# Projecting k and v of the second batch with half of the heads in either column tile of TensorE

## The chip, the cores and the metric

One core of a Trainium2 chip runs the whole program. The metric is the time of one execution in microseconds of device time; medians of several executions are given. "Before" is the kernel as it was, "the changed kernel" the one with the change. One profiled execution of each kernel gives the trace; its span is 1.7 to 1.8 us shorter than the timed figure of the same execution, so spans are compared with spans and times with times.

## The reference

```python
# q, k, v: (8 batches, 8 heads, 1024, 64); E, F: (64, 1024); FFN 512 -> 1536 -> 512
k_proj = einsum('ks,bhsd->bhkd', E, k)            # 64 projected keys per head
v_proj = einsum('ks,bhsd->bhkd', F, v)
attn   = softmax(q @ k_proj^T / sqrt(64))
x      = (attn @ v_proj), heads side by side      # (8192, 512)
out    = (silu(x @ w_gate) * (x @ w_val)) @ w_out # (8192, 512), float32
```

The matrix work is nearly all in the last line. The change is in the first two, for one batch out of eight.

## The kernel before

TensorE's order is written by hand. The feed-forward steps of one half batch (`gps`: gate, `vps`: value, `yps`: output) run in numbered slots; the attention of the *next* batch is put into some slots between them. Batch 0 is done in the prologue, batches 2 to 7 project k and v together, k in the left half of the array's columns and v in the right half. Batch 1 is the exception: its v arrives from memory much later than its k, so each is projected alone.

```python
def u_KV(b, what="kv", hs=(0, H), at="a"):
    ...
    todo = [x for x in (("k", 0, ET, kb), ("v", 64, FT, vb)) if x[0] in what]
    for j in range(NJ):                                   # 8 pieces of the sequence
        for _, lo, w, src in todo:
            nc.tensor.matmul(
                out=t[lo : lo + 64, h0:h1].rearrange("p h d -> p (h d)"),
                lhsT=w[:, j, :],                          # 128 x 64: half of the columns
                rhs=src[b][:, h0:h1, j, :],               # 8 heads x 64 = 512 columns
                start=(j == 0), stop=(j == NJ - 1),
            )
    if "k" in what:
        nc.scalar.copy(out=ks[b % 2][0:64, h0:h1], in_=t[0:64, h0:h1])
    ...                                                   # v: two VectorE copies into BDV

def u_KT(b, at="a", prs=(0, NPAIR)):                      # k' turned: 4 products of 64 columns
    for pr in range(*prs):
        nc.tensor.matmul(out=t[:, pr, :],
            lhsT=ks[b % 2][:, 2 * pr : 2 * pr + 2, :].rearrange("p h d -> p (h d)"),
            rhs=ident_bf[:, 0:KP], start=True, stop=True)
    ...                                                   # copies into the block diagonal BD

def u_TD(b, ch):                                          # q transposed by a DMA
    nc.sync.dma_start_transpose(out=t[:], in_=qb[b, ch][:].rearrange("p h j d -> p (h j d)"))
...
    if b == 1:
        put(22, u_TD, 1, 0)
        put(29, u_KV, 1, "k")
        put(32, u_KT, 1)
        put(40, u_KV, 1, "v")
        sa = (35, 36, 37, 38, 41, 42, 43, 44)             # slots of the scores
```

The prologue's loads go through GpSimd's DMA queue in program order:

```python
    load_v(0, (0, 4, 6, 8))
    load_w_gv(0, 1)            # gate and value weights, first block of 128 columns
    ...
    load_w_gv(10, 12)
    load_q(1, 0)
    load_k(1)
    load_wo(0)
    load_wo(1)
```

The softmax here doesn't subtract the row's maximum and nothing guards it: scores larger than these inputs give would overflow.

Of the kernel before, what the change touches and what calls it, by code (L numbers as in the profile page):

```python
# [12 lines left out]
BF16 = mybir.dt.bfloat16  # L13
FP32 = mybir.dt.float32
# [4 lines left out]
D = 64  # L19
# [3 lines left out]
P = 128  # L23
NJ = S // P
NPAIR = H // 2
# [9 lines left out]
def kernel(  # L35
# [19 lines left out]
    nc = tc.nc  # L55
    scale = 1.0 / float(D) ** 0.5

    const = ctx.enter_context(tc.tile_pool(name="const", bufs=1))
# [13 lines left out]
    ident_bf = const.tile([P, P], BF16, name="ident_bf")  # L72
    ident_fp = const.tile([P, P], FP32, name="ident_fp")
    BD = [const.tile([P, H, P], BF16, name=f"BD{i}") for i in range(2)]
    BDV = [const.tile([P, NPAIR, P], BF16, name=f"BDV{i}") for i in range(2)]
    ks = [const.tile([P, H, D], BF16, name=f"ks{i}") for i in range(2)]
    ET = const.tile([P, NJ, KP], BF16, name="ET")
    FT = const.tile([P, NJ, KP], BF16, name="FT")

# [4 lines left out]
    kb, vb, qb, xT, hT = {}, {}, {}, {}, {}  # L84
# [45 lines left out]
    kvp = {}  # L130
    banks = {"a": (ps_a, "pa"), "g": (ps_g, "gps"), "v": (ps_v, "vps"), "y": (ps_y, "yps")}

    def bank(where, shape, dt, name):
        pool, tag = banks[where]
        return pool.tile(shape, dt, name=name, tag=tag)

    def copy(eng, out, in_):
        (nc.scalar.copy if eng is nc.scalar else eng.tensor_copy)(out=out, in_=in_)  # L138

    def u_KV(b, what="kv", hs=(0, H), at="a"):  # L140
# [5 lines left out]
        h0, h1 = hs  # L146
        todo = [x for x in (("k", 0, ET, kb), ("v", 64, FT, vb)) if x[0] in what]
        for j in range(NJ):
# [15 lines left out]
        if h1 == H:  # L164
            kvp.pop(key)

    def u_V0(p0, p1, at):

        t = bank(at, [P, p1 - p0, P], FP32, "kvp")
        nc.tensor.matmul(  # L170
            out=t[:].rearrange("p a d -> p (a d)"),
            lhsT=zeros[:, 0:P], rhs=zeros[:, 0 : (p1 - p0) * P],
            start=True, stop=False,
        )
        src = vb[0][:].rearrange("p (a c) j d -> p a c j d", c=2)
        for j in range(NJ):
            for c in range(2):
                nc.tensor.matmul(
                    out=t[64 * c : 64 * c + 64, :, 64 * c : 64 * c + 64],
                    lhsT=FT[:, j, :],  # L180
                    rhs=src[:, p0:p1, c, j, :],
                    start=False,
                    stop=(j == NJ - 1),
                )
        nc.scalar.copy(out=BDV[0][:, p0:p1, :], in_=t[:])

    def u_V0w(p0, p1, at):
# [10 lines left out]
        for c in range(2):  # L198
            rows = slice(64 * c, 64 * c + 64)
            nc.scalar.copy(out=BDV[0][rows, p0:p1, rows], in_=t[64:P, :, c, :])  # L200

    def u_KT(b, at="a", prs=(0, NPAIR)):




        t = bank(at, [P, NPAIR, KP], FP32, "kTp")
        for pr in range(*prs):
            nc.tensor.matmul(  # L209
                out=t[:, pr, :],  # L210
                lhsT=ks[b % 2][:, 2 * pr : 2 * pr + 2, :].rearrange("p h d -> p (h d)"),
                rhs=ident_bf[:, 0:KP],
                start=True,
                stop=True,
            )
        bd = BD[b % 2][:].rearrange("p (a c) k -> p a c k", c=2)
        for c in range(2):
            src = t[64 * c : 64 * c + 64, slice(*prs)]
            nc.vector.tensor_copy(out=bd[0:64, slice(*prs), c, 0:64], in_=src)
            nc.vector.tensor_copy(out=bd[64:128, slice(*prs), c, 64:128], in_=src)  # L220
# [239 lines left out]
    def put(s, fn, *a):  # L460
        slots[s].append((fn, a))

    def place(b):
        s0 = 48 * (b - 1)
        if b == 1:
            put(22, u_TD, 1, 0)
            put(29, u_KV, 1, "k")
            put(32, u_KT, 1)
            put(40, u_KV, 1, "v")
            sa = (35, 36, 37, 38, 41, 42, 43, 44)  # L470
            put(41, u_AD, 1, 0)
            put(30, u_TD, 1, 1)
            put(47, u_AD, 1, 1)
            sp = (44, 45, 46, 46, 66, 67, 68, 69)
        else:
            put(s0 + (8 if b == 2 else 0), u_KV, b)
            put(s0 + (11 if b == 2 else 3), u_KT, b)
            o = 14 if b == 2 else 6
            put(s0 + (9 if b == 2 else -6), u_TD, b, 0)
            put(s0 + (11 if b == 2 else -4), u_TD, b, 1)  # L480
            sa = [s0 + o + 3 * j for j in range(NJ)]
            put(sa[3] + 4, u_AD, b, 0)
            put(sa[7] + 4, u_AD, b, 1)
            sp = [s0 + i for i in (39, 41, 43, 45, 57, 59, 61, 63)]
        for j in range(NJ):
            put(sa[j], u_S, b, j)
            put(sa[j] + 1, u_R, b, j)
            put(sa[j] + 1, u_N, b, j)
        for i in range(8):
            put(sp[i], u_PV, b, i // 4, i % 4)  # L490
# [5 lines left out]
    with tc.manual_schedule():  # L496
# [3 lines left out]
        for i in range(2):  # L500
            nc.scalar.dma_start(
                out=kraw[i][:],
                in_=k[0, 2 * i : 2 * i + 2].rearrange("h (p j) d -> p h (j d)", j=NJ),
# [12 lines left out]
        def turn(which, at, halves=(0, 1), eng=nc.scalar):  # L516
            for half in halves:
# [7 lines left out]
                js = slice(4 * half, 4 * half + 4)  # L525
                copy(eng, (ET, FT)[which][:, js, :], ps[:])

# [52 lines left out]
        u_A(0, 0, act)  # L580
        u_V0w(0, 2, "y")
        u_V0(2, 3, "v")
        u_PV2(0, 0, 0, 0, act)
        u_A(0, 2, dve)
        u_N(0, 3, dve)
        u_V0(3, 4, "y")
        u_PV1(0, 0, 2, 0, act)
        u_PV1(0, 0, 3, 0, act)
# [35 lines left out]
        for b in range(1, B):  # L624
            place(b)
        for b in range(2, B):
            s0 = 48 * (b - 1) - (20 if b == 3 else 24)
            at = (43, 43, 44, 45) if b == 2 else (s0, s0 + 2, s0 + 4, s0 + 6)
# [10 lines left out]
        for c in range(B * CH - 1):  # L639
            for n in range(NFT):  # L640
                f = n if c else 4 + (2 * n + 1) // 3
                ypart[(c + 1) * NFT + f].append((c, n))

        for t in range(NIT):
            c, f = divmod(t, NFT)
            i = 1 if t < 2 else None
# [39 lines left out]
```

## Time and profile before

| | before |
|---|---|
| time, median of 3 runs | 567.86 us (567.65 to 568.19) |
| span of the profiled run | 565.8 us |
| TensorE busy | 98%, granted clock 1.00 |
| k of batch 1, start to next work | 1.84 us |
| v of batch 1, start to next work | 1.84 us |
| turning k' | 0.11 us |

In a timeline line the first number is the start in us from the span's beginning, the second the length, then engine, source line, operation, tiles written and read, weight block, moving block and count; in brackets is the idle time before it and what ended it. Matmul records overlap, so the cost of a piece of TensorE work is read as the distance from its start to the start of the next. The prediction below shows the lines.

### The profile page before, as it was taken

How to read it: one execution, taken by the hardware profiler on the slowest of the kernel's cores; microseconds unless marked ns; L12 is line 12 of the kernel's file. 1: busy time of each engine (PE TensorE's matmuls, PEld its weight loads, DVE VectorE, ACT ScalarE, POOL GpSimd, SP SyncE). 2: the span in 40 equal slices, each digit the busy share in tenths (PEclk: the TensorE clock that was granted, in tenths of full speed). 3: DMA queues.
4: the chain of work that ended last, by engine and by line, in shares of the span. 5: the costliest groups of instructions: out<-in, count | busy, mean ns of one | idle time of the engine just before them, and what ended most of it. 6: DMA issues, size and time to landing. Idle time of an engine off the chain costs nothing.

```text
span 565.8 us, 7865 instructions
## 1 busy us (share of the span) xinstructions
PE 556.9 (98%) x2904; PEld 266.0 (47%) x2958; DVE 339.6 (60%) x579; ACT 235.7 (42%) x417; POOL 111.9 (20%) x126
## 2 busy tenths in 40 slices
PE   8999999999999999999999999999999999999997
PEld 4654444444444444444444444444444444444444
DVE  3786665766476655765566655666547665545550
ACT  3574352453444433543435434354343542443222
POOL 6860250133012400133002230024100220000000
PEclk9999999999999999999999999999999999999999
DMA  9999989629903795029920399005990213010012
GB/s 206 188 199 188 182 139 204 120 57 199 203 25 75 120 204 105 38 57 172 191 67 37 77 188 201 38 20 112 193 180 19 61 35 74 37 38 33 24 39 93
DMA packets 112215, 62.78 MB, mean 111 GB/s; under 512 B 66352, under 2 KB 103472, under 8 KB 112176
## 3 DMA queue, kind: packets, MB, share of 16 engines
q0 software_dynamic: 43952, 29.49, 36.5%
q1 hardware_dynamic: 67392, 31.46, 25.3%
q10 hardware_dynamic: 832, 1.31, 0.7%
q8 instruction: 23, 0.38, 0.3%
q14 instruction: 16, 0.13, 0.1%
HBM read 60.29 MB, written 16.78 MB: 136 GB/s over the span
## 4 chain that ended last, share of the span: by engine, by line
PE 95%; DMA 3%; issue 1%; ACT 0%; POOL 0%; POOLq 0%
PE vps L395 29%; PE yps L433 29%; PE gps L395 29%; PE kvp L150 3%; PE sc L286 2%; PE pv L343 2%; DMA wg<-in_moe_w_gate_dram 2%; DMA kb<-in_k_dram 2%; PE qTp L252 0%; PE kTp L209 0%; PE yps L395 0%; PE aTp L332 0%; ACT th L407 0%; ACT AT L138 0%; POOL qb L108 0%
## 5 line engine op out<-in xcount | busy, mean ns | idle before, releaser
L414 DVE SCALAR_TENSOR_TENSOR s<-th,gps 128x512 f32<-128x512 f32 x191 | 129.7, 679 | 134.0 <-ACT th L407 133.6
L395 PE MATMUL vps<-xT,wv 128*128 128x512 bf16 (+1 forms) x762 | 196.1, 377 | 0.9
L395 PE MATMUL gps<-xT,wg 128*128 128x512 bf16 (+1 forms) x750 | 193.9, 377 | 1.0
L433 PE MATMUL yps<-wo,hT 128*128 128x512 bf16 (+2 forms) x763 | 191.8, 376 | 0.7
L407 ACT ACTIVATE th<-gps 128x512 f32<-128x512 f32 x191 | 114.0, 597 | 159.9 <-PE gps L395 145.4
L419 DVE TENSOR_TENSOR hT<-s,vps 128x512 bf16<-128x512 f32 x192 | 131.9, 687 | 20.8 <-DVE s L414 0.5
L316 POOL TENSOR_TENSOR AAd<-ee,rr 128x512 bf16<-128x512 f32 x56 | 58.2, 1041 | 342.5 <-issue 221.7
L433 PEld LDWEIGHTS <-hT 128*128 128x128 bf16 x780 | 76.2, 98 | 89.9
L395 PEld LDWEIGHTS <-wv 128*128 128x128 bf16 x776 | 73.8, 98 | 83.6 <-issue 3.2
L395 PEld LDWEIGHTS <-wg 128*128 128x128 bf16 x776 | 74.0, 98 | 81.4 <-issue 0.8
L443 ACT ACTIVATE ysb<-yps 128x512 f32<-128x512 f32 (+1 forms) x65 | 38.4, 590 | 77.7 <-PE yps L433 75.5
L138 ACT CAST xT<-pv 128x512 bf16<-128x512 f32 (+1 forms) x63 | 36.2, 578 | 51.3 <-PE pv L343 50.3
L301 DVE TENSOR_REDUCE zz<-ee 128x8 f32<-128x512 f32 x64 | 43.5, 679 | 22.0 <-ACT ee L290 21.9
L290 ACT ACTIVATE ee<-sc 128x512 f32<-128x512 f32 x64 | 37.9, 596 | 19.1 <-PE sc L286 17.9
L286 PEld LDWEIGHTS <-qTd 128*128 128x128 bf16 x224 | 17.2, 98 | 13.2
L343 PE MATMUL pv<-AT,BDV 128*128 128x512 bf16 x60 | 22.4, 379 | 0.2
L286 PE MATMUL sc<-BD,qTd 128*128 128x128 bf16 x224 | 21.6, 219 | 0.1
L303 DVE RECIPROCAL rr<-zz 128x8 f32<-128x8 f32 x64 | 13.0, 203 | 6.3
L108 POOL DMA_DIRECT2D qb<-in_q_dram x18 | 16.3, 910 | 0.8 <-POOLq L670 0.8
L150 PE MATMUL kvp<-kb,ET 128*64 128x512 bf16 (+1 forms) x72 | 15.5, 358 | 0.0
L162 DVE CAST BDV<-kvp 64x256 bf16<-64x256 f32 x7 | 3.0, 426 | 20.0 <-ACT ks L158 17.8
L150 PE MATMUL kvp<-vb,FT 128*64 128x512 bf16 x56 | 13.4, 382 | 0.0
(74 smaller groups left out, 139.1 us busy)
## 6 DMA issues: line engine op xcount, KB each, us to landing
out_dram<-ysb SPq DMA_DIRECT2D x63, 256.0 KB, 2.3
qb<-in_q_dram POOLq DMA_DIRECT2D x14, 512.0 KB, 17.9
kb<-in_k_dram POOLq DMA_DIRECT2D x7, 1024.0 KB, 11.1
vb<-in_v_dram POOLq DMA_DIRECT2D x7, 1024.0 KB, 14.1
wo<-in_moe_w_out_dram POOLq DMA_DIRECT2D x2, 768.0 KB, 21.5
kraw<-in_k_dram ACTq DMA_DIRECT2D x2, 512.0 KB, 4.8
qb<-in_q_dram POOLq DMA_DIRECT2D x4, 256.0 KB, 7.8
wg<-in_moe_w_gate_dram POOLq DMA_DIRECT2D x4, 256.0 KB, 7.5
```

What stands on the lines that cost most here:

```text
L138: (nc.scalar.copy if eng is nc.scalar else eng.tensor_copy)(out=out, in_=in_)
L150: nc.tensor.matmul(out=t[lo : lo + 64, h0:h1].rearrange("p h d -> p (h d)"), lhsT=w[:, j, :], rhs=src[b][:, h0:h1, j, :], start=(j == 0), ...
L286: nc.tensor.matmul(out=ps[:, n, :], lhsT=t[:, n, :], rhs=BD[b % 2][:, 4 * g + n, :], start=True, stop=True)
L290: nc.scalar.activation(out=e[:].rearrange("p h j k -> p (h j k)"), in_=ps[:].rearrange("p a k -> p (a k)"), func=AF.Exp, scale=scale,)
L301: nc.vector.reduce_sum(out=z[:], in_=e[:], axis=AX.X)
L316: eng.tensor_tensor(out=a.rearrange("p j h k -> p h j k"), in0=ee.pop((b, u))[:], in1=rr.pop((b, u))[:].unsqueeze(3).to_broadcast([P, 4, 2 ...
L395: nc.tensor.matmul(out=ps[:, ts], lhsT=(wg, wv)[w][:, kt, f * P : (f + 1) * P], rhs=x[:, kt, ts], start=(kt == 0), stop=(kt == NKT - 1),)
L407: nc.scalar.activation(out=th[:], in_=ps[:], func=AF.Tanh, scale=0.5)
L414: nc.vector.scalar_tensor_tensor(out=s1[:], in0=th[:], scalar=1.0, in1=g[:], op0=ALU.add, op1=ALU.mult)
L419: nc.vector.tensor_tensor(out=hT[c][:, f, :], in0=s1[:], in1=ps[:], op=ALU.mult)
L433: nc.tensor.matmul(out=yy[c][:, cs], lhsT=hT[c][:, f, i * P : (i + 1) * P], rhs=wo[:, f, cs], start=(f == 0), stop=(f == NFT - 1),)
L443: nc.scalar.activation(out=ysb[:, cs], in_=yy[c][:, cs], func=AF.Copy, scale=0.5)
```

## The change

The eight heads are split into two sets of four. For each piece of the sequence, two matmuls of 256 columns follow each other, one for either set, with the same weights in the left and in the right half of the columns. If the halves run at the same time, a projection takes half as long. The heads of k' then lie on both row halves of a new tile `ksp`, so two products with the full identity turn it.

```diff
--- before.py
+++ after.py
@@ -74,6 +74,7 @@
     BD = [const.tile([P, H, P], BF16, name=f"BD{i}") for i in range(2)]
     BDV = [const.tile([P, NPAIR, P], BF16, name=f"BDV{i}") for i in range(2)]
     ks = [const.tile([P, H, D], BF16, name=f"ks{i}") for i in range(2)]
+    ksp = [const.tile([P, NPAIR, D], BF16, name=f"ksp{i}") for i in range(2)]
     ET = const.tile([P, NJ, KP], BF16, name="ET")
     FT = const.tile([P, NJ, KP], BF16, name="FT")
 
@@ -164,6 +165,39 @@
         if h1 == H:
             kvp.pop(key)
 
+    def u_K1(b, gs=(0, 2), at="a"):
+
+        g0, g1 = gs
+        t = bank(at, [P, 2 * (g1 - g0), D], FP32, "kvp")
+        src = kb[b][:].rearrange("p (g c e) j d -> p g c e j d", c=2, e=2)
+        for j in range(NJ):
+            for c in range(2):
+                nc.tensor.matmul(
+                    out=t[64 * c : 64 * c + 64].rearrange("p (g e) d -> p g e d", e=2),
+                    lhsT=ET[:, j, :],
+                    rhs=src[:, g0:g1, c, :, j, :],
+                    start=(j == 0),
+                    stop=(j == NJ - 1),
+                )
+        nc.scalar.copy(out=ksp[b][:, 2 * g0 : 2 * g1], in_=t[:])
+
+    def u_V1(b, at="a"):
+
+        t = bank(at, [P, NPAIR, D], FP32, "kvp")
+        src = vb[b][:].rearrange("p (a c) j d -> p a c j d", c=2)
+        for j in range(NJ):
+            for c in range(2):
+                nc.tensor.matmul(
+                    out=t[64 * c : 64 * c + 64],
+                    lhsT=FT[:, j, :],
+                    rhs=src[:, :, c, j, :],
+                    start=(j == 0),
+                    stop=(j == NJ - 1),
+                )
+        for c in range(2):
+            rows = slice(64 * c, 64 * c + 64)
+            nc.vector.tensor_copy(out=BDV[b % 2][rows, :, rows], in_=t[rows])
+
     def u_V0(p0, p1, at):
 
         t = bank(at, [P, p1 - p0, P], FP32, "kvp")
@@ -199,13 +233,22 @@
             rows = slice(64 * c, 64 * c + 64)
             nc.scalar.copy(out=BDV[0][rows, p0:p1, rows], in_=t[64:P, :, c, :])
 
+    def turn_ksp(t, b, g):
+        nc.tensor.matmul(
+            out=t[:, 2 * g : 2 * g + 2, :].rearrange("p a k -> p (a k)"),
+            lhsT=ksp[b][:, 2 * g : 2 * g + 2, :].rearrange("p h d -> p (h d)"),
+            rhs=ident_bf[:],
+            start=True,
+            stop=True,
+        )
+
     def u_KT(b, at="a", prs=(0, NPAIR)):
 
 
 
 
         t = bank(at, [P, NPAIR, KP], FP32, "kTp")
-        for pr in range(*prs):
+        for pr in range(*prs) if b > 1 else ():
             nc.tensor.matmul(
                 out=t[:, pr, :],
                 lhsT=ks[b % 2][:, 2 * pr : 2 * pr + 2, :].rearrange("p h d -> p (h d)"),
@@ -213,6 +256,8 @@
                 start=True,
                 stop=True,
             )
+        for g in range(2) if b < 2 else ():
+            turn_ksp(t, b, g)
         bd = BD[b % 2][:].rearrange("p (a c) k -> p a c k", c=2)
         for c in range(2):
             src = t[64 * c : 64 * c + 64, slice(*prs)]
@@ -464,9 +509,9 @@
         s0 = 48 * (b - 1)
         if b == 1:
             put(22, u_TD, 1, 0)
-            put(29, u_KV, 1, "k")
+            put(29, u_K1, 1)
             put(32, u_KT, 1)
-            put(40, u_KV, 1, "v")
+            put(40, u_V1, 1)
             sa = (35, 36, 37, 38, 41, 42, 43, 44)
             put(41, u_AD, 1, 0)
             put(30, u_TD, 1, 1)
```

## The prediction

> **What bounds the kernel now.** I read the page first: the busy shares, then the slices, then the chain that ended last.
>
> ```profile
> span 565.8 us, 7865 instructions
> ...
> PE 556.9 (98%) x2904; PEld 266.0 (47%) x2958; DVE 339.6 (60%) x579; ACT 235.7 (42%) x417; POOL 111.9 (20%) x126
> ...
> PEclk9999999999999999999999999999999999999999
> DMA  9999989629903795029920399005990213010012
> ...
> PE 95%; DMA 3%; issue 1%; ACT 0%; POOL 0%; POOLq 0%
> ```
>
> The reader is to see a core whose TensorE is occupied nearly all the time, at full clock, and whose end is set by TensorE for 95% of the chain; the 3% of DMA lies in the first 21 us (the long pieces of the chain in order of time: k until 10.8 us, a gate weight until 21 us). A busy TensorE is not by itself proof, as its records overlap, so I asked who made it wait. The view of waits, kept to TensorE, names five waits, all before 18 us, 2.6 us together; kept to the time after 52 us it is empty. So a microsecond of TensorE time removed after 52 us is a microsecond off the span, unless some other thing turns out to arrive too late for the earlier TensorE. The 40-slice row of the DMA shows where that could be: the transfer engines are full until some 64 us, just where the change works.
>
> Next the stretch that the change touches: the timeline of TensorE.
>
> ```profile
> 50.29 1.91 PE L150 MATMUL kvp<-kb,ET 128*64 128x512 bf16 x8
> 52.13 1.04 PE L395 MATMUL gps<-xT,wg 128*128 128x512 bf16 x3
> ...
> 54.74 0.28 PE L209 MATMUL kTp<-ident_bf,ks 128*128 128x64 bf16 x4
> 54.85 1.03 PE L395 MATMUL vps<-xT,wv 128*128 128x512 bf16 x4
> ...
> 67.93 1.91 PE L150 MATMUL kvp<-vb,FT 128*64 128x512 bf16 x8
> 69.77 1.04 PE L395 MATMUL vps<-xT,wv 128*128 128x512 bf16 x4
> ```
>
> Columns: start, length of the merged piece (to the end of its last matmul, so pieces overlap), engine, line, operands, weight block, moving block, count. The difference of two starts is what a piece costs: 52.13 - 50.29 = 1.84 us for k of batch 1, 69.77 - 67.93 = 1.84 us for v, 0.11 us for turning k'. Each projection is 8 matmuls of 512 columns whose weight block has only 64 columns: half of the array does nothing.
>
> **What the Trainium skill says.** (1) "TensorE: Matmul & The Clock Gate", Part 3, The mechanism: matmuls with tile positions in different column groups run at the same time, starting a few ns apart. The trace agrees. Batch 2 projects k and v together, one in either half of the columns:
>
> ```profile
> 94.08 0.40 PE L150 MATMUL kvp<-kb,ET 128*64 128x512 bf16 x1
> 94.08 0.40 PE L150 MATMUL kvp<-vb,FT 128*64 128x512 bf16 x1
> 94.32 0.38 PE L150 MATMUL kvp<-kb,ET 128*64 128x512 bf16 x1
> 94.32 0.38 PE L150 MATMUL kvp<-vb,FT 128*64 128x512 bf16 x1
> ```
>
> Pairs start within 0.01 us, and the sixteen last from 94.08 to 95.93, 1.85 us: no longer than the eight of batch 1. (2) The same page, Back-to-back issue gap: 262 cycles for 256 columns and 518 for 512, 109 and 216 ns at 2.4 GHz. The trace agrees at 512 (216 ns between starts above). At 256 the k of batch 0, whose heads come in halves, has it:
>
> ```profile
> 8.10 1.06 PE L150 MATMUL kvp<-kb,ET 128*64 128x256 bf16 x8
> 9.09 0.40 PE L252 MATMUL qTp<-ident_bf,qb 128*128 128x128 bf16 x4
> ```
>
> 9.09 - 8.10 = 0.99 us for eight; with one of them 0.27 us long, the other seven steps take (1.06 - 0.27)/7 = 0.11 us each. (3) "TensorEngine Tiling (Array Packing)", Overview, Key Properties: a change of tiling mode drains the engine. The four matmuls before k start at 49.33 and should give way at 49.33 + 4 x 0.216 = 50.19; k starts at 50.29. So about 0.1 us is lost on entry, in each of the two projections, before and after the change alike. (4) Its Restrictions: column tiling switches off the fast weight load. The trace agrees in the durations: a weight load of 64 columns takes 106 to 110 ns in these groups, one of 128 columns 98 ns. I return to it as a rival.
>
> **The change part by part.** k of batch 1: 8 matmuls of 512 columns go, 16 of 256 come, two by two in the two column tiles. Eight steps of 216 ns become eight steps of 111 ns (the batch 0 row): 8 x 0.105 = 0.84 us saved, 1.84 to about 1.00 us, all on the path. v of batch 1: the same, 0.84 us. Turning k': four matmuls of 64 columns, 0.11 us by the starts (54.85 - 54.74), become two of 128. A step of 128 columns is read from the scores: four cost 60.26 - 60.03 = 0.23 us, 56 ns each, so two are 0.11 us. Saved: 0.0; the new form is there because the heads now lie on both row halves. The sum on TensorE is 2 x 0.84 = 1.68 us.
>
> Beside the path: the ScalarE copy of k' goes from 64x512 (0.58 us at 52.24) to 128x256, which should be about 0.4 us by the 128x256 cast of batch 0 (409 ns). It has until 54.5 us before the turn needs it, so nothing is gained there. The two VectorE copies of v' keep their 64x256 form (0.43 us each); the two copies of the turned k' stay. No transfer, no buffer and no slot of the order changes; counting TensorE's instructions in the built kernels, 28 more (32 come with the projections, 4 go with the turn), with everything else in its order.
>
> **Where the saving meets something that does not move.** After k, TensorE comes 0.84 us earlier to the scores of batch 1, which need q transposed by a DMA.
>
> ```profile
> 40.69 7.11 SPq L264 DMA_TRANSPOSE qTd<-qb  x1
> ...
> 59.82 0.43 PEld L286 LDWEIGHTS <-qTd 128*128 128x128 bf16 x4
> 60.03 0.39 PE L286 MATMUL sc<-BD,qTd 128*128 128x128 bf16 x4
> ```
>
> That transposition was issued at 40.69 and landed 18.8 us later, in a time when the DMA engines are full: 59.5 us. Before the change that was 0.3 us ahead of the first weight load, so the trace shows no wait. After it the weight load would come at 59.82 - 0.84 = 58.98, while nothing in the change brings the transfer forward. I expect a new wait of about 59.5 - 59.0 = 0.5 us, less 0.1 for the weight load that otherwise runs ahead by 0.2 us and can be closer to its matmul: **0.4 us given back**. TensorE's order is fixed, so it is not made up elsewhere.
>
> The later meetings I worked out with a shift of 0.44 us before v and 1.28 us after it. Second q transposition: 65.18 + 4.3 = 69.5, needed at 71.51 - 1.28 = 70.2, enough. Transposition of the attention rows: issued at 69.26 after GpSimd's last product, landing 6.1 us later at 75.4; first needed at 76.72, which becomes 75.44. The issue comes 0.44 us earlier too, as it hangs on scores before v; but the DMA engines are full again from 67 to 73 us, so the landing may move less. Between 0 and 0.4 us; I take 0.05. The second half of the output weights lands at 33.39 + 23.5 = 56.9 and is used from 58.7, then 57.9: enough. v of batch 1 landed at 41.74 + 20.7 = 62.4, needed at 67.5 now: enough. From the loads of batch 2 on (issued from 74.73), issues follow TensorE's progress and everything is shifted alike.
>
> Sum: 567.86 - 1.68 + 0.40 + 0.05 = 566.6 us.
>
> **Rivals.** A: nothing arrives late, the whole 1.68 us is kept: 566.2. For it: the landing is one profiled execution's, and if it were 0.5 us earlier in the timed ones the wait is gone. Against: 0.3 us of room for 0.84 us of advance. B: the halves do not run two at a time, or the sixteen weight loads at about 110 ns bind: 16 x 0.11 = 1.76 us against 1.84, no gain, 567.8. For it: the slower weight load of column tiles. Against: batch 2 hides two per step, and v of batch 0 runs sixteen 64-column matmuls in alternating column tiles in 0.44 us, about 30 ns per pair, so weight loads of different tiles overlap at a far higher rate than is wanted here. C: the wait for q takes all of k's gain (landing half a microsecond later than recorded), or the attention rows take part of v's too: 567.0 to 567.3. D: VectorE or a PSUM buffer becomes the bound where TensorE runs ahead. Against: at both places VectorE stood idle for the projection (2.19 us before the copy of v'), and the copies it waits for now come earlier.
>
> **Range and chances.** Between A (566.2) and C (567.3) lies most of it; the three runs before span 0.54 us, so a median carries perhaps 0.25 us either way. Range 565.9 to 567.5. All of these are within 0.4% of the time before, and 2% would be 11 us: no path in the trace reaches it. Chances: faster by over 2% 0.003, within 2% 0.992, slower by over 2% 0.005.
>
> **What would show it right or wrong.** In the timeline: pairs of 128x256 matmuls starting within 0.01 us, 0.11 us apart, the next gate or value group 1.0 us after the first (B if 1.8). The turn: two matmuls of 128 columns in 0.11 us. In TensorE's waits after 52 us: one new line, scores waiting for the DMA of the transposed q, 0.2 to 0.6 us; if the list stays empty, A holds. Perhaps a second, PV waiting for the transposed attention rows. The sum is wrong if the landing of the first q transposition moves with TensorE, or if a later load loses its place among the transfers and is late for batch 2.

## The result, and the profile after

| | before | changed |
|---|---|---|
| time, median of 4 runs each, same rounds | 568.0 us (567.65 to 568.19) | 566.76 us (566.54 to 566.97) |
| span of the profiled run | 565.8 us | 564.7 us |
| k of batch 1 | 1.84 us | 1.00 us |
| v of batch 1 | 1.84 us | 0.99 us |
| turning k' | 0.11 us | 0.11 us |

The ratio is 0.9979 (95% interval 0.9962 to 0.9996). A ratio is the mean time of one kernel's fast runs over that of the other's in the same rounds, so it is not quite the ratio of the medians. The gain of about 1.2 us is smaller than the 1.68 us of TensorE time removed.

The timeline of TensorE in the changed kernel, at the places shown above for before:

```profile
50.88 1.06 PE L175 MATMUL kvp<-kb,ET 128*64 128x256 bf16 x16
51.88 1.04 PE L440 MATMUL gps<-xT,wg 128*128 128x512 bf16 x3
...
54.48 0.28 PE L237 MATMUL kTp<-ident_bf,ksp 128*128 128x128 bf16 x2
54.59 1.03 PE L440 MATMUL vps<-xT,wv 128*128 128x512 bf16 x4
...
67.67 1.06 PE L190 MATMUL kvp<-vb,FT 128*64 128x256 bf16 x16
68.66 1.04 PE L440 MATMUL vps<-xT,wv 128*128 128x512 bf16 x3
```

Sixteen matmuls take 51.88 - 50.88 = 1.00 us: by the single records the two of a pair start 0.003 us apart, a pair follows the one before after 0.106 us (the first after 0.13), and the gate matmul behind starts 0.205 us after the last pair, so some 0.1 us goes on leaving. The two products of the turn take 0.11 us as the four did. So the work itself shrank as worked out: 0.84 and 0.85 us.

But k starts at 50.88 us, where before it started at 50.29. TensorE lost 0.59 us before it reached the first changed instruction. From the start of k to the projections of batch 2 it is 42.09 us instead of 43.79, the full 1.70 us less; 1.70 - 0.59 is the 1.1 us between the two spans. So in this pair of traces all of the shortfall lies ahead of the change. The waits of TensorE in the changed kernel, longest first (engine, tile and line that waited, what it waited for, us in total, times, longest), show where:

```profile
PE warm L577 <- DVE zeros L555: 1.2, 1, 1.2
PE vps L440 <- DMA wv<-in_moe_w_val_dram: 0.8, 1, 0.8
PE sc L331 <- DVE BD L139: 0.7, 1, 0.7
```

The middle line is new: the first value matmuls waited 0.81 us for their weights, until 20.84 us. The timeline has them in before and then in the changed kernel:

```profile
19.91 0.60 PE L395 MATMUL vps<-xT,wv 128*128 128x256 bf16 x4
```

```profile
20.84 0.61 PE L440 MATMUL vps<-xT,wv 128*128 128x256 bf16 x4 [0.81 <-DMA wv<-in_moe_w_val_dram]
```

And the wait for q that the prediction expected is there, but only on the weight loads (the 0.31 us in the bracket below), where it costs nothing; kept to the time after 52 us, the list of TensorE's matmul waits is empty. The timelines of the weight loads and of TensorE's matmuls around the first scores:

```profile
59.75 0.23 PEld L331 LDWEIGHTS <-qTd 128*128 128x128 bf16 x4 [0.31 <-DMA qTd<-qb]
59.77 0.39 PE L331 MATMUL sc<-BD,qTd 128*128 128x128 bf16 x4
```

The scores would have started at 58.05 + 8 x 0.216 = 59.78 us behind the output products that began at 58.05; they started at 59.77. TensorE came late by itself, and so just in time for q, which was issued at 40.89 and took 18.8 us, landing at 59.7. Two candidates for the missing 0.4 to 0.5 us thus stood side by side: the landing of q (theory W), and the noise of the first 45 us, ahead of the change (theory N). Theory N was later split into P, the late start belongs to the program as built, and C, it is chance from run to run.

### The profile page after: what moved, and what is told of

It is laid out like the page before. It is cut to its first block, busy times and chain, and to the rows that moved or that the text cites. A ratio compares the mean times of both kernels' runs of the same rounds, so it can differ in the third digit from the quotient of the medians.

```text
span 564.7 us, 7892 instructions
## 1 busy us (share of the span) xinstructions
PE 555.2 (98%) x2917; PEld 266.0 (47%) x2972; DVE 339.5 (60%) x579; ACT 235.5 (42%) x417; POOL 111.9 (20%) x126
## 4 chain that ended last, share of the span: by engine, by line
PE 95%; DMA 2%; POOL 1%; issue 1%; ACT 0%; POOLq 0%
PE vps L440 29%; PE yps L478 29%; PE gps L440 29%; PE sc L331 2%; PE pv L388 2%; DMA wv<-in_moe_w_val_dram 2%; PE kvp L151 2%; POOL vb L100 0%; POOL qb L109 0%; PE kvp L175 0%; PE kvp L190 0%; PE qTp L297 0%; PE kTp L252 0%; PE yps L440 0%; POOL kb L90 0%
## 5 line engine op out<-in xcount | busy, mean ns | idle before, releaser
L139 ACT CAST xT<-pv 128x512 bf16<-128x512 f32 (+1 forms) x63 | 36.2, 578 | 52.3 <-PE pv L388 50.3
L151 PE MATMUL kvp<-kb,ET 128*64 128x512 bf16 (+1 forms) x64 | 13.6, 355 | 0.0
L151 PE MATMUL kvp<-vb,FT 128*64 128x512 bf16 x48 | 11.5, 382 | 0.0
```

The costliest lines, as they stand in the source:

```text
L139: (nc.scalar.copy if eng is nc.scalar else eng.tensor_copy)(out=out, in_=in_)
L151: nc.tensor.matmul(out=t[lo : lo + 64, h0:h1].rearrange("p h d -> p (h d)"), lhsT=w[:, j, :], rhs=src[b][:, h0:h1, j, :], start=(j == 0), ...
```

## The experiments

Twelve runs were made, of eleven new kernels and of the changed one again (e5). Each was profiled once and timed in five rounds (e11 has six times) beside before. Every one gave correct results. The 95% interval of a ratio of times is 0.7 us or more wide on either side, so a difference of 0.3 to 0.5 us between two kernels' times proves little by itself; such readings rest on the traces, one execution each. "Packed" means: in the new form.

**One table for all traces.** Three distances make the traces comparable. From the start of batch 2's projections to the end every trace has 471.70 to 471.77 us, so nothing after them matters. From the start of k of batch 1 to there, the kernels differ by what was edited and by waits. And the start of k itself differs. "Fetch" is explained below. PV is the product of the attention rows with v.

| kernel | k starts | k to batch 2 | waits before k, other than those of all traces | waits after k | fetch minus 1024th packet |
|---|---|---|---|---|---|
| before | 50.29 | 43.79 | none | none | +0.10 |
| changed | 50.88 | 42.09 | value weights 0.81 | none | -0.21 |
| e1, k only | 50.35 | 43.37 | none | q, 0.41 | -0.11 |
| e2, v only | 51.21 | 42.94 | value weights 0.85 | none | -0.16 |
| e3, changed, filled | 51.05 | 42.51 | value weights 0.73 | none | -0.22 |
| e4, before, filled | 50.46 | 44.22 | gate weights 0.23 | none | +0.16 |
| e5, changed again | 51.52 | 43.84 | E 1.1, half clock | q, 1.44; PV 0.3 | +0.59 |
| e6, before, padded | 50.66 | 43.78 | none over 0.3 | none | +0.18 |
| e7, k only, padded | 51.59 | 44.33 | E 1.1, half clock | q, 1.39 | +0.85 |
| e8, q early | 50.95 | 42.29 | value weights 0.66 | PV 0.2 | -0.28 |
| e9, changed, other v of batch 0 | 50.88 | 42.09 | value weights 0.93 | none | -0.13 |
| e10, v only, other v of batch 0 | 50.30 | 42.94 | gate weights 0.21 | none | -0.10 |
| e11, both edits | 52.35 | 43.09 | E 2.2, half clock | second q and PV, 1.0 | +0.95 |
| e12, before, finer warming | 51.07 | 43.79 | v of batch 0, 0.78 | none | -2.43 |

Waits after k are the distance to the same piece in a trace without a wait: from the start of k to the first scores it is 8.89 us with k packed, and from v to the first PV 7.94 us with v packed.

**e1 and e2: one half of the change each.** e1 puts v back, e2 puts k and its turn back.

```diff
# e1
-            put(40, u_V1, 1)
+            put(40, u_KV, 1, "v")
# e2
-            put(29, u_K1, 1)
+            put(29, u_KV, 1, "k")
-        for pr in range(*prs) if b > 1 else ():
+        for pr in range(*prs):
-        for g in range(2) if b < 2 else ():
+        for g in ():
```

> Only k of batch 1 (and its turn) packed. Theory W (the landing of the transposed q, near 59.5 to 59.8 us, takes part of k's gain): the trace shows k in 1.00 us instead of 1.84, a weight load of the scores waiting for the DMA of q, and the time falls by about 0.4 us against before. Rival N (the whole 1.68 us counts, and the missing 0.4 us is the noise of the first 45 us): it falls by 0.84 us.

> Only v of batch 1 packed, k and its turn as before. Theory W and rival N both say 0.84 us less than before, since nothing between v and the end is late; so v alone should be worth about twice k alone under W, and the same as k under N.

e1: 567.37 us (567.18 to 567.55) against 567.93 us of before (9 runs): 0.56 us less, ratio 0.9989 (0.9976 to 1.0001): the times alone can't tell 0.4 from 0.84. Its trace shows the wait that was predicted. The timeline of TensorE in e1:

```profile
57.52 1.89 PE L478 MATMUL yps<-wo,hT 128*128 128x512 bf16 x8
59.66 0.40 PE L331 MATMUL sc<-BD,qTd 128*128 128x128 bf16 x4 [0.26 <-DMA qTd<-qb]
59.90 1.03 PE L440 MATMUL gps<-xT,wg 128*128 128x512 bf16 x4
```

The scores could have started at 57.52 + 1.73 = 59.25 us and started at 59.66: 0.41 us lost of the 0.84 us that k gained. (The bracket says 0.26 because the modelled end of the last matmul before is later than the slot in which the next could have begun.) From k to batch 2 it is 43.37 us against 43.79: 0.42 us kept. Theory W is shown in this trace.

e2 was a miss under both theories: 567.63 us (567.35 to 567.69), only 0.30 us less by the medians where 0.84 was due; ratio 0.9993 (0.9980 to 1.0005). In its trace the work is right, 42.94 us from k to batch 2 against 43.79, 0.85 us less. But k starts at 51.21 us, 0.92 us later than in before, and the list of waits again has the first value weights, 0.85 us. So something ahead of every changed instruction differed, and in all five timed runs the gain was short.

**e3 and e4: filling the wait.** Two 512-column matmuls on a tile of zeros stand ahead of the first scores of batch 1, in the changed kernel and in before.

```diff
+        if (b, u) == (1, 0):
+            for _ in range(2):
+                nc.tensor.matmul(out=ps[:].rearrange("p a k -> p (a k)"),
+                    lhsT=zeros[:, 0:P], rhs=zeros[:], start=True, stop=True)
```

> The changed kernel with two idle 512-column matmuls (0.43 us of TensorE) put just ahead of the first scores of batch 1, behind the place where q is waited for in program order. W: they fill the wait, and the time is that of the changed kernel within 0.1 us; the scores no longer wait for q. N: 0.43 us more than the changed kernel.

> The same two idle matmuls in the kernel before: the price of the filling by itself. Both theories: 0.43 us more than before, as TensorE is never late for q there.

e4: 568.61 us (568.18 to 568.72) against 567.93, 0.68 us more by the medians, ratio 1.0011 (0.9998 to 1.0025); in its trace it is 0.43 us more from k to batch 2, and k starts 0.17 us later than in before. e3: 567.26 us (566.79 to 567.53), against 567.93 of before, ratio 0.9986 (0.9974 to 0.9999); the changed kernel itself was not in these rounds. That is 0.67 us under before, where the changed kernel had been some 1.2 us under: the forecast of W, within 0.1 us of the changed kernel, missed. In its trace TensorE came to k at 51.05, so there was no wait to fill and the filling cost its 0.43 us (42.51 against 42.09). The run does not tell the theories apart, as TensorE came late. It says that in runs like this the wait for q is not what costs.

**e5, e6, e7: is the late start a matter of the program or of the run?** The changed kernel and e1, as built, have the same first 877 TensorE instructions and a few more, up to v of batch 1 near 67 us, yet one waited for weights at 20 us and the other didn't.

```diff
# e6 on before, e7 on e1: idle work behind the last real matmul
+        pad = bank("a", [P, CW], FP32, "pad")
+        for _ in range(8):
+            nc.tensor.matmul(out=pad[:, 0:64], lhsT=zeros[:, 0:P], rhs=zeros[:, 0:64],
+                             start=True, stop=True)
```

> The changed kernel once more, unaltered, in the rounds of the next three. The first trace of it showed a wait of 0.8 us at about 20 us for the first value weights, before any changed instruction runs, and so did the traces of the two other kernels with the packed v, while the three without it had none. Theory P (the late landing belongs to the built program): it is there again and the time is 1.2 us under before. Rival C (it is chance from run to run): it is gone in some runs, and the times spread by 0.4 us or more.

> The kernel before with 8 idle 64-column matmuls at its very end, behind the last real one, where TensorE is done and only the last copies and stores run: 16 more TensorE instructions, none of them ahead of the end. If the length of the program moves the early landing (theory P in its form length), the wait at 20 us appears and the time rises by 0.3 to 0.8 us; if not, the time is that of before within 0.1 us.

> k alone packed, with the same 8 idle matmuls at the end: as many TensorE instructions as the changed kernel has, whose first 877 are the same. Length: the early wait appears, k starts at about 51 us instead of 50.35, the wait for q goes away since TensorE comes late by itself, and the time stays near that of k alone plus 0.2 us. Not length: nothing changes against k alone, 567.4 us.

e5, the changed kernel unaltered, gave 568.84, 567.36, 566.64, 566.89 and 567.02 us against a median of 567.97 us of before: median 567.02, 0.95 us less, with a spread of 2.2 us. The profiled run was the longest, and it did *not* wait for the value weights. So chance from run to run decides (C), at least in part. e6 gave 568.27 us (567.85 to 568.55; ratio 1.0004, 0.9991 to 1.0016), e7 567.54 us (567.26 to 569.41). Neither waited for the value weights, though e7 has as many TensorE instructions as the changed kernel (2972 weight loads on the page of each). That speaks against the length of the program as the cause, but with one trace each, and e7's start was another unusual one, it is not shown; whether the 0.3 us of e6 is anything stays open, as the interval holds 1.

The profiled runs of e5 and e7 show theory W at its largest. TensorE waited 1.1 us for E near 6 us and was then granted half the clock for some 3 us; the loads were late too, and in e5 q of batch 1, issued at 42.70 us and taking 19.1 us, landed at 61.8. The timeline of TensorE in e5:

```profile
58.68 2.00 PE L478 MATMUL yps<-wo,hT 128*128 128x512 bf16 x8
61.85 0.40 PE L331 MATMUL sc<-BD,qTd 128*128 128x128 bf16 x4 [1.17 <-DMA qTd<-qb]
```

Here the first scores lost 1.44 us (10.33 us after k instead of 8.89), and PV another 0.3 us: of the packing's 1.70 us nothing was left (43.84 us from k to batch 2, against 43.79 of before).

**What the late weights have to do with.** Counting the DMA packets of the traces one by one, one thing goes with the wait in the first ten traces (up to e8). The queue marked instruction moves 23 packets of 16 KB; the first of them takes 0.89 to 0.95 us in every trace (the later ones 0.88 to 1.9), as long as some twenty of the 256-byte packets of the weights (41 ns). At 256 instructions per packet (the figure is of the Trainium skill, "Runtime: NRT & Kernel Launch", Instruction fetch mechanics) 23 packets are 5,888 instructions, near TensorE's 5,916 in before (its page has 2,958 weight loads, and each goes with one matmul). The first of them comes near 19 us, in the middle of the first weight loads. Let the moment at which the 1024th 256-byte packet has landed, counted from 14 us on (earlier ones belong to other loads), stand for the first gate and value blocks (512 packets each). A fetch that comes first can hold back some of these packets itself, so the measure is not independent of the effect. In the four traces with the wait up to e8, the fetch began 0.16 to 0.28 us ahead of that moment; in the six without it, at most 0.11 us ahead, or later. First the DMA queues of the changed kernel from 18 to 20 us (packets, MB, and the packets' time as a share of 16 engines' time; it exceeds 100% where packets overlap), then the value weights' transfer in before and in the changed kernel (size and us from issue to landing are the last two figures):

```profile
q0 software_dynamic: 1393, 0.34, 176.2%
q8 instruction: 1, 0.02, 3.0%
```

```profile
wv<-in_moe_w_val_dram POOLq DMA_DIRECT2D x1, 128.0 KB, 10.9
```

```profile
wv<-in_moe_w_val_dram POOLq DMA_DIRECT2D x1, 128.0 KB, 12.2
```

One fetch among some 1,400 small packets, and one block of weights issued at the same time (8.55 and 8.56 us) that lands 1.3 us later, while the gate block beside it (10.9 and 10.8 us) does not. The reading (theory F): the fetch holds one of the 16 DMA engines for 0.9 us, and a transfer is not landed until its share on that engine is. If the value weights still have a share behind it, TensorE waits; by the table a few hundredths of a microsecond decide. The traces here don't say which engine a packet used, so this much is an inference, and it was put to the test.

**e8: q loaded earlier.**

```diff
+        load_q(1, 0)
         load_w_gv(10, 12)
-        load_q(1, 0)
         load_k(1)
```

> The changed kernel with the load of batch 1's first q moved ahead of the last third of the gate and value weights, so that its transposition is issued earlier. Theory W: it lands 1.5 us or more before the scores, there is no wait for q, and the distance from the start of k to the projections of batch 2 is 42.09 us whether or not TensorE came late to k; the time is that of the changed kernel where TensorE came late anyway, or 0.3 us less. If the weights then come late instead, a wait on them before 45 us shows and the time rises.

566.84 us (566.59 to 567.05) against 567.97 of before: 1.13 us less, ratio 0.9979 (0.9967 to 0.9992), as the changed kernel. The transposition was issued at 38.33 us and landed 18.8 us later, at 57.1; there was no wait for q. But TensorE came to k at 50.95 after a wait of 0.66 us for the value weights, and lost 0.2 us at PV, where the transposed attention rows (issued near 69 us, 6.8 us to landing) were not in time; the prediction had allowed 0 to 0.4 us there. As TensorE came late by itself, the run does not show what the earlier q is worth.

**e9, e10, e12: moving the fetch.** e9 (on the changed kernel) and e10 (on e2) project one pair of v of batch 0 with 18 fewer instructions; e12 (on before) cuts the warming matmuls in two, which puts some 30 more instructions ahead.

```diff
# e9, e10
-        nc.vector.memset(BDV[0][:, 0:2], 0.0)
+        nc.vector.memset(BDV[0][:, 0:3], 0.0)
-        u_V0(2, 3, "v")
+        u_V0w(2, 3, "v")
# e12
-            for _ in range(n):
+            for i in range(2 * n):
+                cs = slice(256 * (i % 2), 256 * (i % 2) + 256)
                 nc.tensor.matmul(
-                    out=ps[:], lhsT=zeros[:, 0:P], rhs=zeros[:],
+                    out=ps[:, cs], lhsT=zeros[:, 0:P], rhs=zeros[:, 0:256],
```

> The changed kernel with one pair of v of batch 0 projected by 8 matmuls in one column tile instead of 16 in two behind a zeroing one (18 TensorE instructions fewer before 19 us, about the same TensorE time). In the ten traces so far TensorE waited 0.66 to 0.85 us for the first value weights exactly in the four where the 16 KB fetch of TensorE instructions began 0.16 us or more before the 1024th 256-byte packet of the weights had landed. Theory F (the fetch holds one DMA engine and with it the value weights): the fetch comes about 0.5 us later, the wait is gone, k starts at 50.3 to 50.6 us; then theory W says the scores wait for q, starting at 59.6 to 59.8 us as in the changed kernel, and the time is 566.5 to 566.9 us, no better than the changed kernel. Rival (the wait comes of the packed v in some other way): it stays, at 20 to 21 us.

> v alone packed, with the same earlier edit. F: the wait for the first value weights is gone, and since no other wait takes it back here, the time falls from 567.6 us by about 0.4 us or more, to 567.0 to 567.2: the 0.84 us of v that its first run lacked. Rival: 567.6 us again.

> The kernel before with the 15 warming matmuls and the later one cut in two (256 columns each, the same TensorE time, some 30 instructions more before 19 us). F: the fetch comes 0.5 us or more earlier, in the middle of the first weights, a wait of 0.5 us or more for the gate or value weights appears at 19 to 21 us in a kernel that never showed it, and the time rises by 0.3 to 0.8 us. Rival: no wait, same time as before.

e12 is the clear one. The fetch moved from 18.87 to 16.80 us. That is too early for the weights; it fell on the load before them, v of batch 0. Its last piece took 12.0 us to land instead of 10.9. TensorE's longest waits in e12:

```profile
PE warm L533 <- DVE zeros L510: 1.2, 1, 1.2
PE kvp L178 <- DMA vb<-in_v_dram: 0.8, 1, 0.8
```

A wait of 0.78 us for v of batch 0 (in the other traces at most 0.11 us, in e9) appeared in a kernel that had shown none there. The value weights, 11.7 us to landing instead of 10.9, came before TensorE needed them. The time rose to 568.46 us (568.34 to 568.60) against 568.07: 0.39 us more, as expected, though the interval of the ratio (0.9995 to 1.0019) is wide. I had named the weights as the victim, and it was v. That a fetch, moved, moves the late transfer with it, is seen in this one pair of traces; with one execution of each, chance is not excluded.

e9 and e10 failed as interventions: the fetch came at 18.77 us in both, no later than in the changed kernel (18.76) and in e2 (19.05). The second fetch did move, to 35.0 us from 33.2 and 33.5; why the first did not is not known. The two runs fell on either side of the border again, 0.13 us ahead with the wait of 0.93 us (e9) and 0.10 us ahead without one (e10), so the border of the table holds in all thirteen traces whose fetch is near the weights. Their times say this: e9, 566.47 us (566.45 to 566.84) against 568.07, 1.60 us less (ratio 0.9974, 0.9962 to 0.9986), with the weights late and the scores at 59.77 us, the same as in the changed kernel. e10, 567.26 us (566.73 to 567.30), 0.81 us less (ratio 0.9986, 0.9973 to 0.9999): about the 0.84 us of v alone, and its trace has no late value weights. Beside e2's 0.30 us that fits the reading, but the two intervals overlap.

**e11: both edits on the changed kernel.**

> The changed kernel with both late transfers taken out of the way: the early edit of the two runs above, and q of batch 1 loaded one place earlier. F and W together: no wait for the value weights and none for q, k starts at 50.3 to 50.7 us, 42.09 us from there to the projections of batch 2, time 566.0 to 566.5 us, 1.6 us or more under before. If either is wrong, a wait of 0.3 us or more is left in the list and the time stays near 566.8.

566.54 us median of 6 (566.29 to 568.92) against 568.07: 1.53 us less by the medians; ratio 0.9980 (0.9968 to 0.9993), its first run in the mean. That first run is the profiled one and another of the kind of e5: E late by 2.15 us, half clock, second q and PV late by 1.0 us together. So the trace can't show that the waits are gone in the others. The median is at the edge of what was expected and no better than e9's 566.47 of the same rounds. The version is not shown to beat the changed kernel.

## Why the prediction was right, and where it was right by luck

The time, 566.76 us, is within 0.2 us of the 566.6 predicted. Point by point:

- **What bounds the kernel.** Right. TensorE waits for nothing after the first scores of batch 1 in before, and the last 471.7 to 471.8 us are the same to 0.1 us in all fourteen traces, whatever was edited.
- **The halves run at the same time.** Right: 1.00 and 0.99 us instead of 1.84, 0.84 and 0.85 us saved; rival B (weight loads bind) falls. The weight loads still last 106 to 110 ns each, and sixteen of them fit into 0.80 us.
- **The turn and the copies.** Right: 0.11 us as before; the ScalarE copy 0.37 us where 0.4 was expected.
- **0.4 us given back at the scores.** Right in mechanism and size where TensorE reaches k at 50.3 us: 0.41 us in e1. In the changed kernel's own trace it cost nothing, because TensorE was 0.59 us late already: the list of waits after 52 us stayed empty, which the prediction had named as the sign of A, and yet the time was not A's 566.2. The two don't add: with k packed the scores start at the later of k's start + 8.89 us and the landing of q, at 59.5 to 59.9 us in the traces with neither half clock nor an early q. That landing moved with the late start too, but less: by 0.2 us in the changed kernel.
- **0.05 us at PV.** 0 in the changed kernel's trace, 0.2 us in e8; the direction was right, the size open.
- **A reading that was loose.** The lines given for 216 ns between starts are 0.24 us apart, at the entry; the pairs behind them start 0.21 to 0.22 us apart. And of the 1.84 us some 0.1 goes on leaving, which the prediction did not name. Both forms have it, so the sum stands.
- **The step that was missing.** The prediction took k's start, 50.29 us, as fixed, since nothing ahead of it changes. In the traces it lies between 50.3 and 51.2 us even without the three half-clock runs, mostly with the landing of the first weights. The prediction named one profiled execution's landing as its weak point for q, but not for TensorE's own arrival. That the sum fits, 1.68 less about 0.45, is thus partly luck: in some runs it is q that takes time back (e1, e5), in others the late weights, and in the profiled pair it was the late start alone. The share of each in the timed runs can't be read, as only profiled runs have traces.

Open: why the wait for the value weights came in five of the eight profiled runs with v packed (not in e5, e10 and e11) and in none of the six with v in its old form. The TensorE instructions ahead of 20 us are the same in the changed kernel and e1; more instructions at the end (e6, e7) did not bring the wait, though e7's start was unusual. Chance on a border of 0.02 us would do, but is not shown. Nor is it shown that the fetch causes the wait; the one pair of e12 is all there is.

## What to carry to other kernels

When a projection fills only half of the array's columns, splitting its moving side over both column tiles nearly halves its TensorE time, here from 1.84 to 1.00 us for eight matmuls; check beforehand whether the next consumer's data will be there that much earlier. Here q had 0.3 us of room, and of k's 0.84 us e1 kept 0.42: the room, and the 0.1 us by which the weight load could come closer to its matmul. For gains near 1 us, compare traces from a fixed landmark to the end (here 471.7 to 471.8 us in every trace) instead of totals: it separates what the edit did from what the start of the run did.

## What the Trainium skill lacked or had wrong

- "Runtime: NRT & Kernel Launch", Instruction fetch mechanics: the refill in 16 KiB blocks agrees (23 packets of 16,384 bytes, the first 0.89 to 0.95 us long), and its cost is called mostly hidden. What the page lacks is a side effect that these runs suggest and do not prove: beside saturated loads, the fetch went with a transfer landing 1.1 to 1.5 us later and TensorE waiting 0.66 to 0.93 us, and in the one trace in which it came 2.1 us earlier another transfer was late (e12).
- "TensorE: Matmul & The Clock Gate", Part 1: the table there gives an idle window of about 3.4 us before the clock is halved. Here the granted clock fell to 0.50 for some 3 us after TensorE had idled 1.12 us (e5) and 2.15 us (e11) behind its warming matmuls, each time 3.4 us after it had first risen to 1.00; after 0.42 us at the same place and 0.93 us near 21 us (e9) it stayed at 1.00.
- No page read here says what a transposition by DMA takes beside saturated loads: 18.7 to 19.2 us from issue to landing for the first q of batch 1 in all fourteen traces, against 4.3 us for the second in before.
